# Twenty feed-forward chunks on ScalarE and GpSimd instead of nine, and one written order for the whole loop

## The chip, the cores and the metric

The kernel runs on one core of one Trainium2 chip. Its time is that of one execution on the device, in microseconds (us). The engines are named as in the profile: PE is TensorE with PEld its weight loads, DVE is VectorE, ACT is ScalarE, POOL is GpSimd, and SP is SyncE, which here only issues DMAs.

## The reference

```python
# x: 4 x 12416 x 128, inducing: 32 x 128, d_ff = 1536
def mab(q, kv):                       # softmax attention, scale 1/sqrt(128)
    s = scale * (q @ kv.transpose(0, 2, 1))
    s = s - s.max(-1, keepdims=True)
    a = np.exp(s)
    a /= a.sum(-1, keepdims=True) + 1e-09
    return a @ kv
h = mab(I, x)                         # stage 1: 32 inducing rows look at all 12416 rows
y = mab(x, h)                         # stage 2: every row looks at the 32 rows of h
gate = 1.0 / (1.0 + np.exp(-(y @ w_gate)))
out = (gate * (y @ w_val)) @ w_out    # feed-forward with a sigmoid gate
```

## The kernel before

Each of the four batches has 97 columns of 128 rows. They are cut into six groups of 16 columns and one spare column. Stage 2 is never multiplied out to 128 wide rows: h is folded into the two input weights (the tile `hw`), so the feed-forward part reads the attention weights themselves. A group's attention weights, normalised and copied four times along the partitions, are `a2n`; a transposing DMA issued on SP turns them into `a2r`, from which PE works.

The feed-forward work is cut into 97 blocks of 512 rows (24 to a batch, and one of the spare columns) and every block into 12 chunks of 128 hidden units. A chunk on its usual way needs: two matmuls with 32 rows of contraction, for the gate (`g_ps`) and for the value (`v_ps` or `vm_ps`); on ACT a tanh of the gate into a ring of 16 chunks (`issue_gate`, L1162; the sigmoid is half of one plus the tanh of half the input); on DVE one instruction that makes u = (tanh + 1) * value (`product`, L1350); and four matmuls of u with the output weights that add into `acc_ps` (`out_mm`, L1248). ACT scales each finished block into `o32` (L1273) and SP writes it out. PSUM has room for one gate tile of two chunks (tag g2), one of one chunk (g1), and for the values the tile v2 and the tile `vm` with two banks each, used in turn. The second bank of `vm` (tag m) is lent to everything else: scores, sums and folds of the stages for later groups and for the next batch.

A chunk that is set aside does not pass DVE: ACT takes the tanh (`gate_take`, L1211) and copies the value out of PSUM (`value_take`, L1216), and POOL adds one (L1213) and multiplies (L1218). The table `ASIDE` lists nine such chunks, all in the last batch. For a group of stage 2, ACT copies the scores (L688), POOL finds the maximum and subtracts it (`s2_lower_pool`), ACT takes the exponential `e` (L712), and POOL adds (L720), inverts (L744 and three more) and spreads (`a2n`, L766).

The order of the work comes from two places. The string `ORDER` is a list of words: g issues the gate of two chunks or of one, in strict turn; V or W the values; x a product; o a number of output matmuls; p, a and d run the oldest waiting side step on PE, ACT or DVE. Which side steps wait there, and when, is decided by the tables `TIMES` and by `turn_page`, which looks at due positions as the chunks advance; steps on POOL, loads and SP's DMAs are issued as soon as they are due. Each engine then runs its instructions in the order in which they were issued.

Of the kernel before, what the change touches and what calls it, by code (L numbers as in the profile page):

```python
# [53 lines left out]
WIDE, FULL, NARROW = "128x32", "128x128", "32x128"  # L54
NEXT = "the slot behind"
RING = 16
ORDER = """
ggVxgVxpgpVxgo4gVd0xo4Vxgo12Vxgo4ggVxo8a0gVxo4Vxgo12Wxa0ggVxo12gWxo4gVxo4go4Vxgo4gVxpVxgo8pa0gVx
gVxo12Vxa0gpVd0xgo16a0gVxo8gWxo4ggVxo4Wxgo8gVxo8Vxa0ggpo8Vd0xga0gVxo16gVxo4Wxgo8gVxo12a0gWxgo12g
Vxo4pa0gVxo4pa0gVxo8gWxo8Vxgo4gWxo8a0gVxgo12gWxo4go4gVxo4pgVxo4pVxa0go8gWxo12Vxa0gVxgpo4gVd0xo4V  # L60
xgo4go8Vxa0go8gWxo8gVxo4go4pgVxpVxo4a0a0ggWxo8gVxo8gVxpo4gVd0xo4Vxgo4go8Vxa0go12Wxa0gVxgo8pa0gVd
0xo12a0gVxo4gVxo12pVd0xgo8gWxo4a0ggVxo12pVxgpgVxo12a0gVxo4gVxo4pgVxo4pVxa0go12Wxa0gVxgo12VxgpgVd
0xo4Vxgo20Vxa0ggWxo12Vxa0ggo4pVxgo4pgVxo4Vxgo12Vxa0go8gWxo4go4gVxo8a0gVxpgVd0xo8a0gVxo12Vxa0go8p
Vxa0go4gVxo8pgVxpVxa0go8a0gWxVxgo12pgVxo4pgVxo4a0gVxo12gVd0xo4pVxa0go12Vxa0gWxgo12gVxo4go4pgVxpa
1gVxo8a0gWxo8Vxgo12a0gWxgo8Vxgo8gWxo8gVxo4go4Vxgo4gVxo12Vxa0ggVxo8gVxo8Vxa0ggVxo12Vxgo4gVxo4pgVd
0xo8Vd0xgo4a0ggVxpVxpo8a0gVxo8gWxo8gVxgo12gWxo12a0gVxgVxpo8a0gVxo4gVxo8gVxo4gWxo4go8gVxo4Wxgo8a0
ggVxo12gWxo4gVxo8gWxo8Vxa0ggo12pVxo4a0a0gVxgWxo8go4gVxo8gWxo4go4gVxo8gWxo12a0gVxgo8Wxgo8gVxo8gpg
VxpVxgo8a0gVxo4gVxo12Wxa0ggVxo16gWxo8Vxgo4ggWxo8gVxo12a0gVxgo4Vxgo8gWxo8gVxo8a0ggWxo16VxgWxo4a0g
gVxo12gWxo4go4Vxgo8gWxgo8gVxo4Vxgo8Vxa0gpVxgo8pa0gVxo12gWxo4gVxo8go4gWxo12a0gVxgpo8Vd0xgo8Vxa0go
4Wxgo4Vxgo8gWxo4go8gVxo4Vxa0gpgo12Vd0xga0gVxo8Vxgo4Wxgo8gVxo4gpVxpa0gVxgo12Wxa0gVxgo16pa0gVxo4gV  # L70
xpo8a0gVxgVxo8gWxo4Vxgo8a0ggWxo16gVxo4pgVxo4pVxa0go4Wxgo8gVxo12pa0gVd0xgo12a0gVxo12gWxgVxo8ggWxo
8gVxo8Vxa0gpgo8Vd0xVxgo4go8Vxa0go12WxggVxo16pVxa0gpVxa0go12gWxo12Vxa0gVxgo8pgVd0xo4a0gVxo8pgVd0x
o4a0ggWxo12gVxo4pgVxo4pVxa0go4Wxgo8ggVxo8pgVxo4pVxo4a0a0ggWxo8gVxo4gVxpo4gVd0xo4Vxgo20Vxa0ggWxo8
a0gVxgo8pVd0xgo8Vxa0go8Vxgo12gVxo8pVxgo4Vxa0a0gWxgo12gVxo12pa0gVxpgVxo12a0gVxo4gVxo8pa0gVxpgVxo8
a0gVxo8gVd0xo4po4a0gVxo4gVxo8Wxgo4gVxo8a1gWxgo12gVxo4gpVxpVxa1go4Wxgo4go8a0gVxo8gWxo8a0gVxgo12Vx
ggVxo12gWxo4Vxgo8gVxo12Vxa0ggVxo12Vxa0go4Vxgo8gVxo4VxgpgVd0xo4gVd0xo16Vxa0gpgVxo8pa0gVxo8Vxgo8Vx
go4Vxgo8gVxpVxa0go12Vxa0gWxgo12Vxgo4go4gWxo4Vxgo8go4gWxo4Vxgo8a0ggWxo12Vxgo4gWxo4gVxo12a0gWxgo16
# [12 lines left out]
Vxo8a0gWxgo4Vxa0go8Wxgo12gVxo4go4pa0gVxo4gVxo4Wxo8a0gVxgo12Wxgo4gVxgo8gWxgo8gVxo4Wxgo12Vxa0ggo4p  # L90
Vxpo4a0gVxo8Wxgo4go4gVxo4pVxa0go8gVxo12a0gWxgVxo12Wxgo8go4gVxo4pa0gVxo8Vxgo12Wxa0gVxgo20a0gWxgo8
Vxgo8Wxgo4gVxo8a0ggWxo12gVxo8pVxa0go4gVxo4Vxgo8gVxgVxo12a0gVxpVxgo8pa0gVxo12gVxo4gVxVxgo8pa0gVxo
4gVxo12Vxa0gVxgo12Vxgo4Vxgo8gVxpa0gVxo12gVxo12a0gWxVxgo20a0gVxgVxo4Vxgo4gVxgo8gWxo12Vxa0gWxgo8go
8gVxo4pVxgo4pVxa0go8gVxo4gVxo12Wxa0gVxgo12gWxo4go4gVxo8go4gWxo4Vxgo4gWxo8a0ggVxo12gWxo8gVxo8a0gW
xgo20Vxa0gpa0gVxo8Vxgo4gWxo8go4gVxo4Wxgo4Vxgo4ggVxo12Vxa0gpVxo4po4a0gVxgo8Wxgo8gVxo4pa0gVxo8Vxgo
12Wxa0gVxgo12pVxa0go4gVxo4gWxo4go4Vxgo8gWxo12a0gVxgo12a0gWxo8gVxo12pa0gVxo4gVxo8Vxgo4a0gVxgVxo12
gVxo4Vxgo4gVxpa0gVxo12gVxo4Vxgo12Vxa0ggVxo12gVxo8Vxgo4gVxpa0gVxo12gVxo8gVxo4a0gVxgVxo12gVxo4gVxp
o8a0gVxo4gVxo8gVxo4Vxgo8a0ggVxo12Wxgo8gVxo4Vxgo8pa0gVxo4Vxgo12a0gVxWxgo12Vxgo4go4pVxgo4a0gVxo4Vx
go8VxgVxgo12Vxa0gpa0gVxo20gVxVxpo12a0gVxgo12Vxgo4Vxa0ggVxo12VxgpVxgo8a0gVxo4gVxo12VxgVxgo12Vxa0g
Wxgo12Vxgo4go8gWxo8Vxgo4gVxgo12Vxa0ggVxo12VxgVxgo8gVxpa0gVxo12gVxo4Vxgo12Vxa0gVxgo16Vxo12Vxo4Vxo  # L100
16
# [4 lines left out]
def kernel(  # L106
# [49 lines left out]

    def x_load(b, s, first=()):
        c0, n = groups[s]
        if s == 0:
            c0, n = 0, n + NLO  # L160
        if b not in xn:
            xn[b] = xnp.tile([P, NCH, C], F16, tag="xn", name=f"xn_{b}")
        cuts = [c0, *(c0 + k for k in first), c0 + n]
        for c, e in zip(cuts, cuts[1:]):
            nc.gpsimd.dma_start(xn[b][:, c:e, :], xv[b, :, c:e, :])
# [125 lines left out]

    def on(what, i, besides=()):
        if vm:
# [10 lines left out]
    side = {"used": 0}  # L304
# [15 lines left out]
    def side_tile(shape, dtype, name):  # L320
        side["used"] += 1
        return bank("m", shape, dtype, name)

    def side_done():
        side["used"] -= 1

    summed = [0] * B
    sums, heads = {}, {}
# [10 lines left out]
    agenda, errands = [], []  # L339
# [5 lines left out]
    def errand(b, at, do):  # L345
        errands.append((b, at, do))
# [98 lines left out]
    def plan_stage1(b, s, score, *total):  # L445
        st = {}
        full = groups[s][1] == GC
        first, second, keep = total
# [29 lines left out]
        n = 512 if full else P  # L478
        if full:
            scores = chain(  # L480
                b - 1,
                (score, "take", fill, WIDE, n),
                (None, "dve", lambda: s1_max(b, s, st["s1"]), n),
# [959 lines left out]
```

## Time and profile before

| | |
|---|---|
| median of 3 runs | 716.03 us (715.92 to 716.07) |
| span of the profiled execution | 714.0 us |
| PE / PEld busy | 682.8 / 402.9 us |
| DVE busy | 698.2 us, 773 instructions |
| ACT busy | 678.0 us, 1019 instructions |
| POOL busy | 444.9 us, 718 instructions |
| granted TensorE clock, mean | 0.998 |

The span runs from the first to the last instruction of the program. The profile gives no other time of that execution; the median of the runs is 2.0 us above its span. A busy time is the union of the instructions' own durations, and consecutive instructions on one engine overlap in the records, so that the distance from one start to the next is often shorter than a duration.

### The profile page before, as it was taken

Reading aid. Unit: us, or ns where it says so; the run is one execution under the profiler, and the core shown is the slowest. Engines: PE = TensorE matmul, PEld = TensorE weight load, DVE = VectorE, ACT = ScalarE, POOL = GpSimd, SP = SyncE. Lnnn points to the kernel's source line nnn. Section 1 sums busy time; section 2 is a strip of 40 time slices with the busy share of each in tenths; the row PEclk is TensorE's granted clock in tenths of the full one; section 3 lists DMA queues with packets and bytes.
Section 4 is the critical chain, followed back from the end, with each engine's and each line's share of the span. In section 5 each row is a group of like instructions: output and inputs, shape, how many; then the busy total and the mean of one; then the engine's idle time right before and its main releaser. Section 6 shows DMA issues by size and latency. Waiting matters only on the chain. (4 is left out here: it accounts for less than half of the span.)

```text
span 714.0 us, 21196 instructions
## 1 busy us (share of the span) xinstructions
PE 682.8 (96%) x8446; PEld 402.9 (56%) x8446; DVE 698.2 (98%) x773; ACT 678.0 (95%) x1019; POOL 444.9 (62%) x718
## 2 busy tenths in 40 slices
PE   7899999999999999999999999999999999999997
PEld 4455565555555655555555555555555555555555
DVE  6899999999999999999999999999999999999997
ACT  4699999999999999999999999999999999999996
POOL 4574663788763747578766366378767787676220
PEclk9999999999999999999999999999999999999999
DMA  9797776244468353225258532220222222023011
GB/s 209 117 173 138 145 142 112 75 91 107 89 125 172 65 119 84 68 75 122 50 130 156 113 76 55 66 75 32 77 61 43 77 62 76 30 76 77 31 45 46
DMA packets 118179, 65.74 MB, mean 92 GB/s; under 512 B 101408, under 2 KB 102208, under 8 KB 118080
## 3 DMA queue, kind: packets, MB, share of 16 engines
q1 hardware_dynamic: 112176, 50.90, 29.9%
q0 software_dynamic: 5584, 13.34, 11.3%
q8 instruction: 66, 1.08, 0.7%
q14 instruction: 33, 0.27, 0.1%
q10 hardware_dynamic: 320, 0.15, 0.1%
HBM read 27.80 MB, written 25.43 MB: 75 GB/s over the span
## 5 line engine op out<-in xcount | busy, mean ns | idle before, releaser
L1162 ACT ACTIVATE t<-g_ps 128x1024 f16<-128x1024 f32 (+1 forms) x770 | 588.6, 821 | 14.5 <-ACT t L1162 2.8
L1350 DVE SCALAR_TENSOR_TENSOR u<-t,v_ps 128x1024 f16<-128x1024 f16 (+1 forms) x337 | 407.6, 1210 | 1.5 <-PE v_ps L1121 0.3
L1248 PE MATMUL acc_ps<-wo,u 128*128 128x128 f16 x4596 | 363.8, 220 | 4.7 <-DVE u L1350 0.7
L1248 PEld LDWEIGHTS <-u 128*128 128x128 f16 x4620 | 263.2, 98 | 153.2 <-issue 146.0
L1350 DVE SCALAR_TENSOR_TENSOR u<-t,vm_ps 128x1024 f16<-128x1024 f16 (+1 forms) x335 | 307.7, 919 | 0.8 <-issue 0.2
L1121 PE MATMUL g_ps<-a2r,hwt 32*128 32x512 f16 (+1 forms) x1179 | 287.8, 375 | 6.9 <-ACT t L1162 0.8
L1121 PEld LDWEIGHTS <-hwt 32*128 32x128 f16 x2382 | 99.3, 91 | 118.1 <-issue 48.4
L1121 PE MATMUL v_ps<-a2r,hwt 32*128 32x512 f16 (+1 forms) x687 | 129.3, 373 | 4.6 <-DVE u L1350 2.9
L1121 PE MATMUL vm_ps<-a2r,hwt 32*128 32x512 f16 (+1 forms) x492 | 129.6, 376 | 4.1 <-DVE u L1350 2.8
L720 POOL TENSOR_TENSOR sum<-e 128x256 f32<-128x256 f16 (+1 forms) x23 | 15.5, 672 | 122.9 <-ACT e L712 119.5
L766 POOL TENSOR_TENSOR a2n<-e,rs 128x2048 f16<-128x2048 f16 (+3 forms) x25 | 86.8, 3473 | 5.1 <-DVE rs L738 3.4
L744 POOL TENSOR_TENSOR near<-sme,minus 128x16 f32<-128x16 f32 (+1 forms) x22 | 65.2, 2964 | 1.7
L1273 ACT ACTIVATE o<-acc_ps 128x512 f32<-128x512 f32 x96 | 57.9, 604 | 0.1
L699 POOL TENSOR_SCALAR rise<-rise 128x256 f32<-128x256 f32 (+6 forms) x110 | 51.0, 464 | 9.7
L698 POOL TENSOR_TENSOR rise<-sc 128x256 f32<-128x256 f32 (+1 forms) x22 | 16.3, 739 | 27.5 <-ACT sc L688 27.5
L700 POOL TENSOR_TENSOR top<-top,rise 128x128 f32<-128x128 f32 (+3 forms) x88 | 28.3, 322 | 7.3
L720 POOL TENSOR_TENSOR sum<-sum 128x128 f32<-128x128 f32 (+3 forms) x92 | 28.3, 307 | 7.2
L698 POOL TENSOR_TENSOR rise<-top 128x128 f32<-128x128 f32 (+3 forms) x88 | 27.2, 309 | 6.9
L1218 POOL TENSOR_TENSOR xn_spare<-xn_spare 128x512 f16<-128x512 f32 x9 | 11.4, 1269 | 22.9 <-ACT xn_spare L1216 22.7
L1213 POOL TENSOR_SCALAR xn_spare<-xn_spare 128x512 f32<-128x512 f16 x9 | 13.4, 1490 | 18.8 <-ACT xn_spare L1211 18.7
L703 POOL TENSOR_TENSOR sc<-sc,top 128x512 f32<-128x512 f32 (+1 forms) x22 | 23.9, 1084 | 1.7
L651 PE MATMUL vm_ps<-hT,xT 128*128 128x32 f16 x376 | 17.5, 177 | 0.5 <-DVE u L1350 0.3
(165 smaller groups left out, 327.3 us busy)
## 6 DMA issues: line engine op xcount, KB each, us to landing
out_dram<-o SPq DMA_DIRECT2D x96, 256.0 KB, 2.3
xn<-in_x_dram POOLq DMA_DIRECT2D x18, 512.0 KB, 6.1
xn<-in_x_dram POOLq DMA_DIRECT2D x3, 544.0 KB, 6.4
xn<-in_x_dram POOLq DMA_DIRECT2D x3, 256.0 KB, 12.3
xn<-in_x_dram SPq DMA_DIRECT2D x1, 576.0 KB, 4.8
xn<-in_x_dram SPq DMA_DIRECT2D x1, 512.0 KB, 3.8
a2r<-a2n SPq DMA_TRANSPOSE x29, 4.8
wg<-in_moe_w_gate_dram POOLq DMA_DIRECT2D x1, 384.0 KB, 12.0
```

The costliest lines, as they stand in the source:

```text
L698: nc.gpsimd.tensor_tensor(out=r, in0=far, in1=near, op=ALU.subtract)
L699: nc.gpsimd.tensor_scalar_max(out=r, in0=r, scalar1=0.0)
L700: nc.gpsimd.tensor_tensor(out=top[:, 0:n, 0:w], in0=near, in1=r, op=ALU.add)
L703: nc.gpsimd.tensor_tensor(out=sc[:, 0:n, :], in0=sc[:, 0:n, :], in1=top[:, 0:n, 0:1].to_broadcast((P, n, m)), op=ALU.subtract,)
L720: nc.gpsimd.tensor_tensor(out=d[:, 0:n, :], in0=src[:, :, 0:w], in1=src[:, :, w : 2 * w], op=ALU.add)
L744: nc.gpsimd.tensor_tensor(out=near[:, 0:n], in0=sme[:, 0:n], in1=minus1[:, 0:n], op=ALU.pow)
L766: eng.tensor_tensor(out=a2n[:, 0:n, :, :], in0=e.unsqueeze(2).to_broadcast((P, n, 4, m)), in1=rs.unsqueeze(2).unsqueeze(3).to_broadcast((P ...
L1121: made_mm.append(nc.tensor.matmul(out[:, col : col + nb * P], hw[b][r : r + 32, j // 2, :], a2r[r : r + 32, o : o + nb, :].rearrange("p j ...
L1162: i = nc.scalar.activation(out=ring[:, p : p + n, :], in_=g[:, 0:n, :], func=AF.Tanh, scale=0.5)
L1248: mm = nc.tensor.matmul(acc[0][half][:, i, :], u[:, ts(i, P)], wo16[:, j, :], start=(i in fresh), stop=not left[ib] and not any(e[1] == ib ...
L1273: nc.scalar.mul(out=o32[:], in_=bank_[:], mul=0.5)
L1350: x = nc.vector.scalar_tensor_tensor(out=u[:, 0:n, a:e], in0=ring[:, p : p + n, a:e], scalar=1.0, in1=v[:, 0:n, a:e], op0=ALU.add, op1=ALU ...
```

## The change

Twenty chunks are set aside instead of nine: two in the first batch (blocks 2 and 10), three in the second (24, 31, 35), four in the third (50, 58, 59, 71), eleven in the fourth (75, 79 twice, 84, 86, 90, 91 three times, 95 twice). Before, the nine were in blocks 75, 79 twice, 86, 91 three times and 95 twice. The room that ACT and POOL need for them is taken from the tile of x that is loaded two batches later (`x_room`), and in the last two batches from a spare tile of that size.

`TIMES`, the agenda and `turn_page` are gone. Every side step, DMA and load belongs to a numbered chain, and the word k with its number runs the next step of that chain at that place. The word b does the same in the one-chunk gate bank g1 instead of bank m; twelve steps do so. The gate words are g for two chunks and h for one, in any turn. The word e scales a finished block on ACT, and f on DVE; there are 95 e and one f.

```diff
-ASIDE = {3: ((-1, 'm', 7, 'm', 3), (11, 'm', 17, 'm', 7), ...
-TIMES = (
...
+ASIDE = (
+    2, 10, 24, 31, 35, 50, 58, 59, 71, 75, 79, 79, 84, 86, 90, 91, 91, 91, 95, 95,
 )
...
-ggVxgVxpgpVxgo4gVd0xo4Vxgo12Vxgo4ggVxo8a0gVxo4Vxgo12Wxa0ggVxo12gWxo4gVxo4go4Vxgo4gVxpVxgo8pa0gVx
...
+gk0k0k0hVxVghxVxgo8Vho4xVgxVhk0o4xVgxo4Vhk72xo8gk74k0Vxo8hWo4xgVo8xehVk110gxo4Vk110k76ho8xVgo8xV
...
     def bank(tag, shape, dtype, name):
+        if tag == "m":
+            tag = here["bank"]
...
-    def chain(b, *steps, needs=()):
-        agenda.append(dict(b=b, steps=list(steps), at=0, name=len(agenda), needs=needs))
-        return agenda[-1]
+    def chain(*steps):
+        chains.append(dict(steps=list(steps), at=0, bank="m"))
+
+    def take_step(k, where):
+        w = chains[k]
+        step = w["steps"][w["at"]]
+        w["at"] += 1
...
     def issue_gate():
-        n, c, thin = units[gate["unit"]], gate["chunk"], gate["unit"] % 2
+        n, c = units[gate["unit"]], gate["chunk"]
+        assert n == 2 or not side["g1"]
...
     def side_room(b):
-        if b == B - 1:
+        if b >= B - 2:
             return spare_room()
-        t = sp.tile([P, 512], F16, tag="side_t", name="side_t", bufs=4)
...
+        if b not in rooms:
+            flat = x_room(b + 2)[:, NCH - 2 * GC :, :].rearrange("p j c -> p (j c)")
...
-        def evacuate():
-            nc.scalar.mul(out=o32[:], in_=bank_[:], mul=0.5)
+        def evacuate(mul):
+            mul(o32[:], bank_[:], 0.5)
             nc.sync.dma_start(ov[b, :, c : c + nb, :], o32[:])
...
-    def turn_page(c):
...
-        elif word == "g":
+        elif word in "gh":
             issue_gate()
...
+        elif word == "e":
+            evac.pop()(lambda out, in_, by: nc.scalar.mul(out=out, in_=in_, mul=by))
+        elif word == "f":
+            evac.pop()(lambda out, in_, by: nc.vector.tensor_scalar_mul(out=out, in0=in_, scalar1=by))
         else:
-            run(later[{"p": "pe", "a": "act", "d": "dve"}[word]].pop(int(k or 0)))
+            take_step(int(k), "m" if word == "k" else "g1")
```

Three places show how the order moves. The first is POOL near the start of the loop, in the first batch, where the weights of the group that begins with block 4 are made. `e`, `sme`, `rs` and `a2n` are that group's tiles, `xn_91` is the x of the second batch that is being loaded. Before:

```order
L720 TENSOR_TENSOR sum_771<-sum_769 128x16
L726 TENSOR_SCALAR sme<-sum_771 128x16
L165 DMA xn_91<-in_x_dram 128x2048 x2
L766 TENSOR_TENSOR a2n<-e,rs 128x2048
L698 TENSOR_TENSOR rise<-sc 128x256
```

Now, with `xn_834` the room of the chunk that is set aside:

```order
L695 TENSOR_TENSOR sum_764<-sum_762 128x16
L701 TENSOR_SCALAR sme<-sum_764 128x16
L1182 TENSOR_SCALAR xn_834<-xn_834 128x512
L160 DMA xn_91<-in_x_dram 128x2048
L1187 TENSOR_TENSOR xn_834<-xn_834 128x512
L741 TENSOR_TENSOR a2n<-e,rs 128x2048
L160 DMA xn_91<-in_x_dram 128x2048
```

Two POOL steps of the set-aside chunk now stand ahead of `a2n`, and one of the two loads has moved from ahead of `a2n` to just behind it.

The second place is POOL in the first batch where the weights for block 12 are made; `xn_1805` and `xn_834` are the x of the third batch, under its number in each program. Before:

```order
L726 TENSOR_SCALAR sme<-sum_1899 128x16
L744 TENSOR_TENSOR near<-sme,minus_132 128x16
L748 TENSOR_TENSOR off<-sme,near 128x16
L751 TENSOR_SCALAR off<-off 128x16
L759 TENSOR_TENSOR rs<-near,off 128x16
L766 TENSOR_TENSOR a2n<-e,rs 128x2048
L165 DMA xn_1805<-in_x_dram 128x2048
```

Now:

```order
L701 TENSOR_SCALAR sme<-sum_2045 128x16
L160 DMA xn_834<-in_x_dram 128x2048
L719 TENSOR_TENSOR near<-sme,minus_132 128x16
L723 TENSOR_TENSOR off<-sme,near 128x16
L726 TENSOR_SCALAR off<-off 128x16
L734 TENSOR_TENSOR rs<-near,off 128x16
L741 TENSOR_TENSOR a2n<-e,rs 128x2048
L1182 TENSOR_SCALAR xn_834<-xn_834 128x512
L1187 TENSOR_TENSOR xn_834<-xn_834 128x512
```

The load that stood just behind `a2n` now stands ahead of the inversion, and the steps of the chunk set aside in block 10 follow `a2n`.

The third place is ACT in the second batch, from the exponential `e` of the group that begins with block 28; `xn_4075` is the room of the chunk set aside in block 24. Before:

```order
L712 ACTIVATE e<-sc 128x512
L1162 ACTIVATE t_621<-g_ps 128x1024
L1162 ACTIVATE t_621<-g_ps 128x512
L1162 ACTIVATE t_621<-g_ps 128x1024
L1273 ACTIVATE o_4126<-acc_ps 128x512
```

Now:

```order
L687 ACTIVATE e<-sc 128x512
L1125 ACTIVATE t_621<-g_ps 128x1024
L1125 ACTIVATE t_621<-g_ps 128x512
L1180 ACTIVATE xn_4075<-vm_ps 128x512
L1125 ACTIVATE t_621<-g_ps 128x1024
L1185 COPY xn_4075<-side_v_ps 128x512
L1326 ACTIVATE o_4118<-acc_ps 128x512
```

Between the same neighbours ACT now takes the tanh and the value of one chunk that DVE would have multiplied.

More of the change, by code (lines that the diff above doesn't have):

```diff
@@ L155, with x_room @@
     xn, xT = {}, {}
+    def x_room(b):
+        if b not in xn:
+            xn[b] = xnp.tile([P, NCH, C], F16, tag="xn", name=f"xn_{b}")
+        return xn[b]
     def x_load(b, s, first=()):
@@ L160, in x_load @@
             c0, n = 0, n + NLO
-        if b not in xn:
-            xn[b] = xnp.tile([P, NCH, C], F16, tag="xn", name=f"xn_{b}")
+        x_room(b)
         cuts = [c0, *(c0 + k for k in first), c0 + n]
@@ L290 @@
     OTHER = {"v1": "m", "m": "v1"}
+    here = {"bank": "m"}
     def on(what, i, besides=()):
-        if vm:
+        if vm and (what != "m" or here["bank"] == "m"):
             me = str(i.ins.engine)
@@ L443, in s1_sum_keep, with plan_stage1 @@
         on("m", nc.scalar.copy(out=hsts[b % 2][0:R, at_col[s], 0:width], in_=hp[0:R, 0:width]))
-    def plan_stage1(b, s, score, *total):
+    def plan_stage1(b, s):
         st = {}
         full = groups[s][1] == GC
-        first, second, keep = total
         def fill():
@@ L476, in put, with most @@
             side_done()
[L478 removed]
+        def most():
+            s1_max(b, s, st["s1"])
         if full:
[L480 to L483, printed above, removed]
[L484 to L502 removed]
+            chain((fill,), most, weigh, turn_dma)
+            chain((lambda: part(0, 2),), lambda: part(2, 4), put)
+        else:
+            chain((fill,), most, weigh, turn_pe, turn_copy)
+            chain((lambda: part(0, 2),), put)
     hT16 = {}
@@ L558, in join_min, with plan_combine @@
         return top
[L560 removed]
+    def plan_combine(b):
         q = b % 2
@@ L624, in take @@
             side_done()
-        heads[b] = chain(
-            b - 1,
-            (lead, "dve", least, 60),
-            (None, "do", meet, 3000),
-            (weights, "act", weigh, 60),
-            (weights + 1, "do", join, 4600),
-            (weights + 8, "take", total, FULL, 640),
-            (None, "dve", invert, 60),
-            (None, "dve give", take, 60),
-            *(
-                step
-                for hf, (first, second) in enumerate(fill)
-                for step in (
-                    (first, "take", lambda hf=hf: part(hf), WIDE, 384),
-                    (None, "act give", lambda hf=hf: keep(hf), 384),
-                )
-            ),
-            needs=[(w, len(w["steps"])) for w in sums[b]],
+        chain(
+            least, meet, weigh, join, (total,), invert, take,
+            *(f for hf in range(2) for f in ((lambda hf=hf: part(hf),), lambda hf=hf: keep(hf))),
         )
@@ L783, in s2_turn_dma, with plan_stage2 @@
             a2[(b, c + j)] = (a2r, j)
-    def plan_stage2(at, b, c, score, take, weigh, far=None, soon=False):
+    def plan_stage2(b, c, far=False, soon=False):
         st = {}
-        n = GC + (NLO if far is not None else 0)
+        n = GC + (NLO if far else 0)
         def room():
@@ L806, in lower @@
         def lower():
-            if far is None:
+            if not far:
                 room()
@@ L1109 @@
     total_chunks = len(chunks)
-    units = []
-    while sum(units) < total_chunks:
-        units.append(min(1 + (len(units) + 1) % 2, total_chunks - sum(units)))
-    base = [b * NG * GC // BC * NJ for b in range(B)]
     def hidden_mm(what, c, out):
@@ L1373 @@
     for b in range(B):
-        more = b + 1 < B
-        times = TIMES[min(b, 1) if more else 2]
         if b == 0:
-            plan_stage2(0, 0, groups[1][0], 0, None, 3, soon=True)
-        for s, (*slots, far) in times["late"].items():
-            plan_stage2(b, b, groups[s][0], *slots, far=far)
-        for n, (g, gb, v, vb, i) in enumerate(ASIDE.get(b, ())):
-            k = sum(e[-1] == i for e in ASIDE[b][:n])
-            i += b * NG * GC // BC
-            plan_aside(b, g, v, i, beyond[i][k])
-        if not more:
+            plan_stage2(0, groups[1][0], soon=True)
+        for s in range(2, NG):
+            plan_stage2(b, groups[s][0], far=s == NG - 1)
+        if b + 1 == B:
             continue
-        for s, slots in enumerate(times["sum"]):
-            plan_stage1(b + 1, s, *slots)
-        plan_combine(b + 1, *times["join"][:2], times["join"][2:])
+        for s in range(NS):
+            plan_stage1(b + 1, s)
+        plan_combine(b + 1)
         for s in range(2):
-            plan_stage2(b, b + 1, groups[s][0], *times["next"][s])
+            plan_stage2(b + 1, groups[s][0])
+    for b in range(B - 1):
         for g in range(NS):
-            errand(b, times["turn"][g], lambda b=b, g=g: x_transpose_dma(b + 1, g))
+            chain(lambda b=b, g=g: x_transpose_dma(b + 1, g))
             if b == 0 and 0 < g < NG:
-                errand(b, (None, 4, 5, 17, 24, 31)[g], lambda g=g: x_load(1, g))
+                chain(lambda g=g: x_load(1, g))
         if b + 2 < B:
             for g in range(NG):
-                when = ((24, 33, 42, 60, 60, 82) if b else (33, 37, 60, 60, 78, 82))[g]
-                errand(b, when, lambda b=b, g=g: x_load(b + 2, g))
+                chain(lambda b=b, g=g: x_load(b + 2, g))
+    for n, i in enumerate(ASIDE):
+        plan_aside(i, beyond[i][ASIDE[:n].count(i)])
     for word, k in words:
@@ L1409 @@
                 out_mm()
-        else:
-            run(later[{"p": "pe", "a": "act", "d": "dve"}[word]].pop(int(k or 0)))
-    assert not queue and not agenda and not errands and not any(later.values())
+        elif word == "e":
+            evac.pop()(lambda out, in_, by: nc.scalar.mul(out=out, in_=in_, mul=by))
+        elif word == "f":
+            evac.pop()(lambda out, in_, by: nc.vector.tensor_scalar_mul(out=out, in0=in_, scalar1=by))
+        else:
+            take_step(int(k), "m" if word == "k" else "g1")
+    assert not queue and not evac and all(w["at"] == len(w["steps"]) for w in chains)
 _INS = ['x', 'inducing', 'moe_w_gate', 'moe_w_val', 'moe_w_out']
```

261 lines of the change are left out of this document (95 added, 166 removed).

## The prediction

> **What bounds the kernel now.** I read the page's busy times first, then the busy time by stretches, then the rows of the engine that is full, and last what it waits for.
>
> ```profile
> span 714.0 us, 21196 instructions
> ...
> PE 682.8 (96%) x8446; PEld 402.9 (56%) x8446; DVE 698.2 (98%) x773; ACT 678.0 (95%) x1019; POOL 444.9 (62%) x718
> ```
>
> Three engines are above 94%, so the mean does not decide. The stretches do (start and end in us, length, then the busy time of each engine):
>
> ```profile
> 30.00:42.00 12.00, 11.41 (x125) 6.20 (x123) 11.56 (x14) 11.46 (x17) 6.61 (x12) 1.00 0.73 142
> 42.00:651.00 609.00, 589.49 (x7298) 348.28 (x7298) 608.20 (x631) 595.87 (x888) 411.52 (x664) 1.00 0.42 91
> 651.00:693.00 42.00, 40.73 (x453) 23.26 (x449) 41.25 (x46) 41.25 (x62) 12.04 (x9) 1.00 0.22 53
> 693.00:714.00 21.00, 16.71 (x255) 11.49 (x255) 16.89 (x20) 14.27 (x22) 1.27 (x1) 0.93 0.14 51
> ```
>
> From 42 to 651 us DVE is idle for 0.8 us in all, PE for 19.5 and ACT for 13.1. So DVE sets the pace there. From 651 to 693 DVE and ACT are equally full. Nearly all of DVE's time is the product, in three shapes; and from start to start a product of two chunks takes 1.13 us (110.40 to 111.53) and one of one chunk 0.60 us (109.80 to 110.40), less than the durations, since records overlap:
>
> ```profile
> L1350 DVE SCALAR_TENSOR_TENSOR u<-t,v_ps 128x1024 f16<-128x1024 f16 x335 | 406.8, 1214 | 1.5 <-PE v_ps L1121 0.3 <-ACT t L1162 0.3 <-PE g_ps L1121 0.2
> L1350 DVE SCALAR_TENSOR_TENSOR u<-t,vm_ps 128x1024 f16<-128x1024 f16 x149 | 181.1, 1215 | 0.3 <-issue 0.2
> L1350 DVE SCALAR_TENSOR_TENSOR u<-t,vm_ps 128x512 f16<-128x512 f16 x186 | 126.7, 681 | 0.4 <-PE vm_ps L1121 0.2
> ...
> 109.80 0.68 DVE L1350 SCALAR_TENSOR_TENSOR u<-t,vm_ps 128x512 f16<-128x512 f16 x1
> 110.40 1.21 DVE L1350 SCALAR_TENSOR_TENSOR u<-t,v_ps 128x1024 f16<-128x1024 f16 x1
> 111.53 1.22 DVE L1350 SCALAR_TENSOR_TENSOR u<-t,vm_ps 128x1024 f16<-128x1024 f16 x1
> ```
>
> The idle columns add up to 2.2 us for 670 products. There is next to nothing to win from waits on DVE; only less work on it helps.
>
> **DVE's work.** Eleven more chunks leave the products: 1155 chunks become 1144. Counted in the two written orders, products of two chunks go from 484 to 479 and those of one chunk from 187 to 186. That is 5 x 1.13 + 0.60 = 6.25 us less. One finished block is scaled on DVE instead of ACT. The nearest row has half its width, and the 512-wide product has its width:
>
> ```profile
> L1265 DVE TENSOR_SCALAR o<-vm_ps 128x256 f32<-128x256 f32 x1 | 0.4, 425 | 0.3 <-PE vm_ps L1248 0.3
> ```
>
> Between 0.4 and 0.7 us; I take the 0.60 of the one-chunk product, from start to start. It is on the path, since DVE is full, and the products behind it on DVE stand while it waits for the block's last output matmul; that matmul stands just ahead of it in the written order, so a wait of up to one product (1.1 us) is possible, and I put none. DVE's net is 6.25 - 0.60 = 5.65 us. What hides everything else is that DVE stays the fullest engine, and this has to be checked for ACT, POOL and PE.
>
> **ACT's work.**
>
> ```profile
> L1162 ACT ACTIVATE t<-g_ps 128x1024 f16<-128x1024 f32 x385 | 397.5, 1032 | 14.0 <-ACT t L1162 2.8 <-PE v_ps L1121 1.2 <-PE vm_ps L1121 0.7
> L1162 ACT ACTIVATE t<-g_ps 128x512 f16<-128x512 f32 x385 | 234.4, 609 | 0.5 <-PE g_ps L1121 0.2
> L1273 ACT ACTIVATE o<-acc_ps 128x512 f32<-128x512 f32 x96 | 57.9, 604 | 0.1
> L1211 ACT ACTIVATE xn_spare<-vm_ps 128x512 f16<-128x512 f32 x9 | 5.4, 602 | 0.0
> L1216 ACT COPY xn_spare<-vm_ps 128x512 f32<-128x512 f32 x9 | 5.3, 593 | 0.0
> ```
>
> Eleven more chunks cost a tanh and a copy each, 11 x (602 + 593) ns = 13.1 us. The usual tanhs become 386 of two chunks and 372 of one: 1.03 us more and 13 x 609 ns = 7.9 us less. One scaling goes, 0.6 us. The net is 5.6 us by durations. ACT is busy for 662.9 us of the 684 between 30 and 714 us (the four stretches above added); with 5.6 us more in 5.65 us less it would be at 98.5%, below DVE's. By starts it is further from full: of the rows
>
> ```profile
> 698.06 0.60 ACT L1273 ACTIVATE o<-acc_ps 128x512 f32<-128x512 f32 x1
> 698.54 4.19 ACT L1162 ACTIVATE t<-g_ps 128x1024 f16<-128x1024 f32 x5
> ```
>
> the first has a duration of 0.60 us and its successor starts after 0.48. So I take ACT's work as hidden, and price its failure as a rival. In the last batch, where ACT and DVE are equal, only two of the eleven new chunks lie.
>
> **PE and SP.** PE has the same matmuls in both programs, and switches between matmuls of 32 and of 128 rows less often (1344 runs of one shape before, 1274 now). Its cost is nil if DVE paces; if PE paces, nothing is won, a rival below.
>
> [...]
>
> ```profile
> L1213 POOL TENSOR_SCALAR xn_spare<-xn_spare 128x512 f32<-128x512 f16 x9 | 13.4, 1490 | 18.8 <-ACT xn_spare L1211 18.7
> L1218 POOL TENSOR_TENSOR xn_spare<-xn_spare 128x512 f16<-128x512 f32 x9 | 11.4, 1269 | 22.9 <-ACT xn_spare L1216 22.7
> ...
> 315.00:336.00 21.00, 20.59 (x241) 12.25 (x239) 21.00 (x26) 20.54 (x31) 19.35 (x25) 1.00 0.50 103
> 378.00:399.00 21.00, 20.32 (x265) 12.13 (x261) 21.00 (x24) 20.52 (x32) 7.58 (x17) 1.00 1.03 184
> ...
> L1350 DVE SCALAR_TENSOR_TENSOR u<-t,v_ps 128x1024 f16<-128x1024 f16 x12 | 14.5, 1210 | 0.0
> L1350 DVE SCALAR_TENSOR_TENSOR u<-t,v_ps 128x1024 f16<-128x1024 f16 x11 | 13.4, 1214 | 0.0
> ```
>
> POOL gets 11 x (1490 + 1269) ns = 30.4 us more and goes from 445 to 475 us, two thirds of the span. As an engine it has room. It could slow DVE beside it: but with POOL busy for 19.35 of 21 us the two-chunk product took 1210 ns (first of the last two rows), and with POOL busy for 7.58 of 21 us it took 1214 ns (second). So the added POOL work costs the products nothing. [...]
>
> **Order on POOL and the weights of the next group.** Here the change can add a wait. PE's first gate of a group needs `a2r`, which lands after e on ACT, 10 us on POOL and a transposing DMA on SP. PE runs in order, so a late `a2r` holds the values behind it too, and DVE then has at most the product whose values stand in the other PSUM tile, 1.13 us, before it stands. Three places in the first half are tight:
>
> ```profile
> 84.27 0.71 PE L1121 MATMUL g_ps<-a2r,hwt 32*128 32x512 f16 x3
> 74.78 5.19 SPq L777 DMA_TRANSPOSE a2r<-a2n  x1
> a2r<-a2n SPq DMA_TRANSPOSE x1, 7.6
> ...
> 113.95 0.39 PE L1121 MATMUL g_ps<-a2r,hwt 32*128 32x512 f16 x2
> 104.40 0.64 POOL L165 DMA_DIRECT2D xn<-in_x_dram  x1
> 104.49 6.01 SPq L777 DMA_TRANSPOSE a2r<-a2n  x1
> a2r<-a2n SPq DMA_TRANSPOSE x1, 9.3
> ...
> a2r<-a2n SPq DMA_TRANSPOSE x29, 4.8
> ...
> 30.36 1.22 DVE L1350 SCALAR_TENSOR_TENSOR u<-t,v_ps 128x1024 f16<-128x1024 f16 x1 [0.27 <-ACT t L1162]
> 709.01 0.75 DVE L1350 SCALAR_TENSOR_TENSOR u<-t,v_ps 128x384 f16<-128x384 f16 x2
> ```
>
> For block 8 the DMA was issued at 74.78 and landed 7.6 us later, at 82.4; the first gate ran at 84.3. For block 12 it landed at 104.49 + 9.3 = 113.8 us, 0.15 us ahead of the gate. Both were slower than the median of 4.8 us; for block 12 the row of POOL shows a load of x issued just ahead. DVE needs 0.59 us for a chunk (679 us from its first product at 30.4 to its last at 709.8, over 1155 chunks). Now, counted in ACT's written order:
>
> - Block 8: between its e and its first gate stand 31 chunks, not 36. That is 2.9 us less time, with a load behind `a2n` as before: 1.9 - 2.9 = -1.0 us.
> - Block 12: 29 chunks, not 34, so 2.9 us less, and 0.64 us for the load that now stands ahead of the inversion. But that load is then out of the way: at 4.8 us instead of 9.3 us the result is 0.15 - 3.5 + 4.5 = +1.1 us; if the DMA is slow all the same, -3.4 us.
> - Block 4: POOL now does the chunk's two steps first. The value is copied 20 chunks (11.8 us) ahead of the first gate; the copy, the multiplication and `a2n` (0.59 + 1.27 + 3.61 us, the last from the row below) leave 6.3 us for the DMA, +1.5 us at 4.8 us and -3.0 us at 9.3 us, since a load now follows `a2n` directly.
> - Block 44: 34 chunks, not 37, and a load directly behind `a2n`; the DMA was issued at 331.97, took 5.1 us to land and the gate ran at 339.42. So 2.3 - 1.8 = +0.5 us, or -3.7 us at 9.3 us.
>
> ```profile
> 331.97 3.62 SPq L777 DMA_TRANSPOSE a2r<-a2n  x2
> a2r<-a2n SPq DMA_TRANSPOSE x2, 5.1
> 339.42 0.39 PE L1121 MATMUL g_ps<-a2r,hwt 32*128 32x512 f16 x2
> 43.04 3.61 POOL L766 TENSOR_TENSOR a2n<-e,rs 128x2048 f16<-128x2048 f16 x1 [1.43 <-DVE rs L738]
> ```
>
> The ends are 0 (all in time, or covered by the 1.13 us) and 1.0 + 3.4 + 3.0 + 3.7 = 11.1 us. Most terms lie near the good end, so I take 1.0 us.
>
> **The sum.** Against the profiled execution: 714.0 - 6.25 + 0.60 + 1.0 = 709.35 us of span. The median of the runs, 716.03, lies 2.0 us above that span, and I keep the 2.0: 711.4 us, 4.65 us or 0.65% less. The difference that a measurement of this kernel can tell from none is about 0.2%, 1.4 us: faster means below 714.6, slower above 717.5.
>
> **Rivals.**
>
> 1. *Late weights (slower).* The mechanism is the one above: with POOL's steps and loads moved, the first gates of blocks 4, 8, 12 and 44 find no `a2r`, PE stands, and DVE with it. At the full price it is 716.03 - 5.65 + 11.1 = 721.5; with half of it covered, 716. It decides from 7.1 us on (5.65 + 1.4). For it: 0.15 us of room at block 12 before. Against it: other groups gain room in the same count (block 32: 45 chunks, not 33).
> 2. *ACT becomes the bound in the last batch.* There ACT had no less to do than DVE (41.25 us each of 42). Its two new chunks save DVE 2 x 0.57 us to no use and cost ACT 2 x 1.195 less two halves of 1.03, 1.4 us; with as much again for the crowded stretch ahead: 716.03 - 5.65 + 1.1 + 2 x 1.4 = 714.3. For it: from 651 to 693 us ACT is idle for only 0.75 us. Against it: starts closer than durations, and gates that now run further ahead of the products (on average 2.7 to 3.5 chunks in the last 160 products, not 1.8 to 2).
> 3. *PE paces and DVE only looks full.* PE is at 589.49 of 609 us. Then the time stays at about 716. Against it: DVE's idle time, 0.8 us in 609.
> 4. *POOL holds up DVE.* If each added POOL instruction held DVE for half its length, 15.2 us: 716.03 - 5.65 + 15.2 = 725.6. The 1210 and 1214 ns speak against it. [...]
> 5. *More than forecast:* no late weights, and the 0.75 us of DVE's idle time from 651 to 693 goes too: 716.03 - 5.65 - 0.75 = 709.6, with a cheaper scaling 709.
>
> **How the numbers follow.** Forecast 0.60 (709.5 to 713.5); late weights 0.16, half of it within 0.2% and half slower; ACT 0.12, mostly still faster (0.10 and 0.02); PE 0.05 (0.04 same, 0.01 slower); POOL 0.03 (0.02 slower, 0.01 same); more than forecast 0.04. That makes 0.74 faster, 0.15 same, 0.11 slower. The likeliest case gives 711.4. The range runs from 708.8, below rival 5, to 716.6, where some 0.12 lies above and little below.
>
> **What the changed profile would show.** DVE's products: 479 and 186, some 6.8 us less busy, with idle time between 42 and 690 us still below 2 us; that is the forecast. PE waiting on the DMA of `a2r`, with idle DVE beside it near 57, 83, 112 or 335 us, is rival 1. ACT without gaps while DVE waits for its tanh in the last 100 us is rival 2. DVE idle throughout, with PE full, is rival 3; a two-chunk product of clearly more than 1215 ns is rival 4. A time above 714.6 would make the prediction wrong.

## The result, and the profile after

The kernel after takes 744.7 us in the median, where 711.4 was forecast; against the kernel before it is 1.041 times as long (95% interval 1.039 to 1.044). Two of its six runs, 755.2 and 759.0 us, are slow ones at a mean granted clock of 0.950 and 0.941, and the median, the ratio and all differences below go by the other four (742.2 to 750.3 us; the median of all six is 748.0). The granted clock is the share of TensorE's full speed that the profile records as granted. The profiled execution is the 743.7 us one, with a span of 741.8 us. The top of its page:

```profile
span 741.8 us, 21216 instructions
...
PE 688.7 (93%) x8446; PEld 403.2 (54%) x8446; DVE 697.3 (94%) x768; ACT 681.8 (92%) x1028; POOL 475.8 (64%) x740
```

The span grew by 27.8 us. None of the three full engines got that much work (POOL did, 30.9 us, but it is busy for 64% only); all three have idle time. Where it lies is seen in the stretches of the kernel after (start and end in us, length, busy time of each engine, granted clock, DMA share, GB/s):

```profile
42.00:63.00 21.00, 15.68 (x181) 8.66 (x179) 16.31 (x19) 15.52 (x24) 15.35 (x22) 0.94 0.78 132
63.00:84.00 21.00, 20.46 (x250) 11.97 (x247) 18.82 (x19) 19.22 (x29) 8.73 (x11) 0.90 0.62 118
84.00:105.00 21.00, 16.88 (x179) 9.05 (x176) 14.66 (x16) 14.32 (x22) 9.13 (x19) 0.76 0.79 138
105.00:126.00 21.00, 19.89 (x278) 12.31 (x278) 20.91 (x26) 20.83 (x34) 14.93 (x17) 1.00 0.86 78
126.00:147.00 21.00, 16.46 (x152) 8.68 (x150) 11.89 (x13) 11.89 (x18) 6.18 (x16) 0.59 0.48 78
147.00:168.00 21.00, 18.49 (x273) 11.00 (x270) 18.98 (x22) 18.64 (x31) 16.97 (x34) 1.00 0.53 114
357.00:378.00 21.00, 18.64 (x193) 10.63 (x189) 17.97 (x18) 17.94 (x27) 14.60 (x28) 0.84 0.50 96
...
42.00:651.00 609.00, 568.70 (x6988) 332.90 (x6986) 579.07 (x595) 571.33 (x854) 415.50 (x653) 0.97 0.43 88
651.00:693.00 42.00, 40.43 (x465) 23.41 (x466) 41.82 (x45) 41.63 (x63) 31.22 (x37) 1.00 0.29 65
```

The third busy time is DVE's. From 42 to 651 us it is idle for 29.9 us, where it was 0.8 before; 27.5 of these lie in the seven short stretches shown, six of which lie ahead of 168 us. In five of them the granted clock is below 1.0, down to 0.59; before it was 1.00. From 651 to 693 us DVE is as full as it was.

What PE waited for in it (total in us, times, longest):

```profile
PE g_ps L1082 <- DMA a2r<-a2n: 12.0, 5, 4.5
...
PE vm_ps L376 <- DMA xT<-xn: 4.9, 1, 4.9
```

And from its timeline four of these waits (in brackets), with issues of DMAs ahead of them:

```profile
50.13 0.59 POOL L160 DMA_DIRECT2D xn<-in_x_dram  x1
50.21 5.48 SPq L752 DMA_TRANSPOSE a2r<-a2n  x1
55.79 3.24 SPq L169 DMA_TRANSPOSE xT<-xn  x1
61.16 0.62 PE L376 MATMUL vm_ps<-xT,indT 128*32 128x512 f16 x4 [4.86 <-DMA xT<-xn]
61.84 0.69 DVE L388 TENSOR_REDUCE nm<-vm_ps 128x1 f32<-128x512 f32 x1 [4.69 <-PE vm_ps L376]
...
84.56 0.64 POOL L160 DMA_DIRECT2D xn<-in_x_dram  x1
85.11 7.23 SPq L752 DMA_TRANSPOSE a2r<-a2n  x1
95.27 0.61 PE L1082 MATMUL g_ps<-a2r,hwt 32*128 32x512 f16 x2 [3.95 <-DMA a2r<-a2n]
...
120.81 9.20 SPq L752 DMA_TRANSPOSE a2r<-a2n  x1
132.09 0.61 PE L1082 MATMUL g_ps<-a2r,hwt 32*128 32x512 f16 x2 [4.54 <-DMA a2r<-a2n]
...
366.69 0.39 PE L1082 MATMUL g_ps<-a2r,hwt 32*128 32x512 f16 x2 [1.16 <-DMA a2r<-a2n]
```

At 61 us PE waits for `xT`, whose transposition stood in SP's queue behind a turn of weights that took 5.48 us to issue. At 95, 132, 167 (1.93 us) and 367 us it waits for the turned weights of blocks 8, 12, 16 and 44. These five stands (idle time of PE ahead of something late) add up to 16.4 us. With four of them the clock is halved: in the trace's record of it, it is 0.5 for 6.83 us from 60.40, for 10.24 us from 94.53, for 17.07 us from 128.67 and for 6.83 us from 367.60, 41.0 us in all. (The last microseconds of each execution, where the clock falls as well, to 0.5 from 711.2 us on before and from 739.7 us on in the kernel after, are left out in this and in all that follows.) In the row at 95.27 a gate matmul takes 0.61 us, where the same at full clock takes 0.39 (the last row).

How long the turns (the transposing DMAs from `a2n` to `a2r`) that are issued from 45 to 200 us take to land, in the median:

```profile
a2r<-a2n SPq DMA_TRANSPOSE x6, 8.9
```

And the same stretch of the kernel before:

```profile
a2r<-a2n SPq DMA_TRANSPOSE x7, 5.8
```

DVE's products, by shape:

```profile
L1269 DVE SCALAR_TENSOR_TENSOR u<-t,v_ps 128x1024 f16<-128x1024 f16 x332 | 402.9, 1214 | 6.3 <-PE v_ps L1082 3.2 <-PE g_ps L1082 2.1
L1269 DVE SCALAR_TENSOR_TENSOR u<-t,vm_ps 128x1024 f16<-128x1024 f16 x147 | 178.3, 1213 | 9.8 <-PE vm_ps L1082 7.0 <-PE g_ps L1082 2.1 <-ACT t L1125 0.2
L1269 DVE SCALAR_TENSOR_TENSOR u<-t,vm_ps 128x512 f16<-128x512 f16 x185 | 125.8, 680 | 9.4 <-PE vm_ps L1082 7.1 <-PE g_ps L1082 0.8 <-ACT o L1326 0.7
```

The work did go down as counted: 479 products of two chunks, 7.6 us less busy, each as long as before. From the start of the first product to the end of the last DVE takes 707.1 us instead of 679.4. If each of its instructions is counted at its usual (median) time from start to start, the work in this is 6.2 us less and the waiting 33.9 us more (40.2 instead of 6.3). That is the whole change: 33.9 - 6.2 = 27.7 us.

### The profile page after: what moved, and what is told of

Read it like the earlier page. It is cut to its first block, busy times and chain, and to the rows that moved or that the text cites. A ratio compares the mean times of both kernels' runs of the same rounds, so it can differ in the third digit from the quotient of the medians.

```text
span 741.8 us, 21216 instructions
## 1 busy us (share of the span) xinstructions
PE 688.7 (93%) x8446; PEld 403.2 (54%) x8446; DVE 697.3 (94%) x768; ACT 681.8 (92%) x1028; POOL 475.8 (64%) x740
## 4 chain that ended last, share of the span: by engine, by line
PE 44%; ACT 23%; DVE 10%; DMA 10%; issue 7%; POOL 5%; DVEq 0%; ACTq 0%; SPq 0%; POOLq 0%
PE acc_ps L1211 21%; ACT t L1125 18%; PE g_ps L1082 11%; DVE u L1269 9%; DMA a2r<-a2n 7%; PE v_ps L1082 5%; PE vm_ps L1082 4%; ACT o L1326 2%; DMA xn<-in_x_dram 2%; POOL a2n L741 2%; POOL near L719 1%; DMA xT<-xn 1%; POOL xn L160 1%; PE vm_ps L376 1%; ACT e L687 1%
## 5 line engine op out<-in xcount | busy, mean ns | idle before, releaser
L1269 DVE SCALAR_TENSOR_TENSOR u<-t,v_ps 128x1024 f16<-128x1024 f16 x334 | 403.7, 1209 | 6.3 <-PE v_ps L1082 3.2
L1211 PEld LDWEIGHTS <-u 128*128 128x128 f16 x4576 | 267.2, 99 | 152.2 <-issue 147.4
L1269 DVE SCALAR_TENSOR_TENSOR u<-t,vm_ps 128x512 f16<-128x512 f16 (+1 forms) x332 | 304.2, 916 | 19.2 <-PE vm_ps L1082 14.1
L1082 PEld LDWEIGHTS <-hwt 32*128 32x128 f16 x2360 | 94.7, 91 | 140.5 <-issue 64.0
L1182 POOL TENSOR_SCALAR xn_spare<-xn_spare 128x512 f32<-128x512 f16 x15 | 22.4, 1494 | 25.4 <-ACT xn_spare L1180 25.3
L1187 POOL TENSOR_TENSOR xn_spare<-xn_spare 128x512 f16<-128x512 f32 x15 | 19.0, 1269 | 27.1 <-ACT xn_spare L1185 26.6
L673 POOL TENSOR_TENSOR rise<-top 128x128 f32<-128x128 f32 (+3 forms) x88 | 27.3, 310 | 6.9
L388 DVE TENSOR_REDUCE nm<-vm_ps 128x1 f32<-128x512 f32 (+1 forms) x21 | 13.1, 626 | 5.2 <-PE vm_ps L376 5.1
```

The lines of the kernel that those rows point to most:

```text
L673: nc.gpsimd.tensor_tensor(out=r, in0=far, in1=near, op=ALU.subtract)
L1082: made_mm.append(nc.tensor.matmul(out[:, col : col + nb * P], hw[b][r : r + 32, j // 2, :], a2r[r : r + 32, o : o + nb, :].rearrange("p j ...
L1211: mm = nc.tensor.matmul(acc[0][half][:, i, :], u[:, ts(i, P)], wo16[:, j, :], start=(i in fresh), stop=not left[ib] and not any(e[1] == ib ...
L1269: x = nc.vector.scalar_tensor_tensor(out=u[:, 0:n, a:e], in0=ring[:, p : p + n, a:e], scalar=1.0, in1=v[:, 0:n, a:e], op0=ALU.add, op1=ALU ...
```

## The experiments

Theory A: the turns of weights and the transposition behind one of them are late because loads of x are in flight beside them, and PE's stands cost their own length and a halved clock besides. Rival B: with twenty chunks set aside, POOL and ACT are too slow, and the loads are only seen beside it. Rival C: the halved clock costs nothing, since DVE is the bound.

**Seven loads moved.** Only words of the written order change place (k78, k84, k85, k86, k87, k88, k101 are loads of x; each now stands behind a tree of maxima on POOL):

```
- o8 k78 k1      + o8 k1 k78        - V k84 k2 k82 g   + V k2 k82 k84 g
- o4 k2 k85 x    + o4 k2 x ... k3 k85 h
- x k87 k86 k20  + x k20 ... k5 k87 k86 x
- o4 h k88 o8    + o4 h o8 ... k21 k88 o8
- x k101 k43 g   + x k43 k101 g
```

> Only the written order is changed: seven loads of x on POOL's queue, each of which stands right behind a spreading of weights (`a2n`) or a sum ahead of one, go behind the tree of maxima that follows, so that none is in flight while the weights of blocks 4, 8, 12, 16, 20 and 44 are turned by DMA. Theory A (the turns are late because a load of x is in flight beside them): the turns of `a2r` fall from 7.2-11.2 us between issue and landing to some 4.4 us, the waits of PE for `a2r` and `xT` (16.4 us in five stands) nearly vanish, the granted clock stays at 1.0 from 10 us to the end, and the time is 709 to 716 us. Rival B (POOL and ACT with twenty chunks set aside are themselves too slow, the loads are only seen beside it): the turns are issued as late as now and the time stays at 735 to 745 us.

Measured: 715.4 us, 0.999 of before (0.998 to 1.001), in the medians 29.4 us less than the kernel after. The turns issued from 45 to 200 us:

```profile
a2r<-a2n SPq DMA_TRANSPOSE x7, 4.4
```

The turn of block 8 in the timeline, with the loads that now follow it:

```profile
78.70 2.10 SPq L751 DMA_TRANSPOSE a2r<-a2n  x1
86.73 1.18 POOL L159 DMA_DIRECT2D xn<-in_x_dram  x2
```

And the stretch around that block's first gate:

```profile
84.00:105.00 21.00, 20.21 (x280) 12.35 (x278) 21.00 (x25) 20.79 (x33) 11.09 (x19) 1.00 0.84 154
```

The turns take 4.4 us and not 8.9, none is waited for, and DVE is full for all 21 us around block 8, which had 6.3 us of idle time. All twenty chunks are still set aside and POOL runs the same instructions. So the first half of A holds, the loads and the late turns, and B falls. The seven were moved together; the next two runs try one each. The clock is still halved once, for 6.83 us from 270.34, where no stand is longer than 0.41 us. Of ten runs the five with a mean clock of 1.0 took 713.8 to 714.7 us, the five at 0.993 to 0.996 took 716.0 to 718.2.

**One load moved.** Of the above only `o8 k78 k1` to `o8 k1 k78`, ahead of block 4.

> Only the first of those loads moves: the fourth group of batch 1, 0.08 us ahead of the turn for block 4, goes behind the tree. Theory A: the turn issued at 50.2 us lands in some 4.4 us and not 9.2, the transposition of `xT` queued behind it on SP lands 4 to 5 us earlier, PE's stand of 4.86 us ahead of 61.2 us and the 6.8 us of halved clock behind it go, and the others stay: 742 - (4.7 + 1.8 us of idle time of DVE) = about 735 us. Rival B: no change, 740 to 745 us.

Measured: 738.7 us, 1.031 of before (1.029 to 1.034). In its trace the turn at 49.57 us lands after 4.4 us, the stand for `xT` falls from 4.86 to 0.76 us and the clock holds up to 86 us; from 42 to 63 us DVE is busy for 20.30 us and not 16.31. The gain is 6.0 us in the medians, where 6.5 was expected. But the stands at blocks 8 and 12 grew to 4.66 and 4.82 us and the slow stretch behind the second from 17.1 to 27.3 us, so the stretches were not as independent as I had them.

**One load put back.** The order with the loads moved, but `V k84 k2 k82 g` as in the kernel after.

> The order with the seven loads behind the trees, and one of them put back: the first load of batch 2 stands again right behind the spreading of block 8's weights. Theory A: the turn of block 8 alone takes some 10 us again, PE stands about 4.5 us at its gate near 85 us, the clock is halved for 7 to 10 us there, and nothing else changes, since blocks 12 and 16 had 2.8 and 2.1 us of room: 714.4 to 715.4 + 5 to 7 = 719 to 722 us. Rival D (the lateness adds up over several loads and stands, one alone is covered): 714 to 717 us.

Measured: 721.7 us, 1.009 of before (1.007 to 1.011), 6.3 us more than with it moved. From its timeline:

```profile
77.72 0.64 POOL L159 DMA_DIRECT2D xn<-in_x_dram  x1
78.28 7.60 SPq L751 DMA_TRANSPOSE a2r<-a2n  x1
...
89.43 0.61 PE L1081 MATMUL g_ps<-a2r,hwt 32*128 32x512 f16 x2 [4.95 <-DMA a2r<-a2n]
```

How long that turn took to land, and then, as another view, the stretch:

```profile
a2r<-a2n SPq DMA_TRANSPOSE x1, 11.1
```

```profile
84.00:105.00 21.00, 15.86 (x152) 8.64 (x149) 13.69 (x17) 13.31 (x21) 3.91 (x10) 0.76 1.09 115
```

One load, issued 0.56 us ahead of one turn, makes it 11.1 us long instead of 4.4, PE stands for 4.95 us, the clock is halved for 10.24 us from 87.71, and DVE loses 7.3 us of the 21. Rival D falls: one alone is not covered.

**Idle matmuls in place of the waits.** In the kernel after:

```
+ for _ in range(FILL.get(c, 0)):
+     nc.tensor.matmul(g[:, 0, :], ident[:], wo16[:, 0:4, :], start=True, stop=True)
  for k in range(n):
      hidden_mm("g", c + k, g[:, k, :])
```

> The order of the kernel after, with idle matmuls for PE in place of the five waits: 22 matmuls of 512 columns ahead of the scores that wait for `xT` at 61 us, and 18, 20, 8 and 5 ahead of the first gates of blocks 8, 12, 16 and 44; each writes a bank that the real matmul behind it overwrites. The DMAs stay as late as they are. Theory A with the clock (a stand of PE of some microseconds halves the granted clock for 7 to 17 us and that costs as well as the wait): the clock stays at 1.0, DVE's idle time behind the waits (1.8, 1.2, about 4.5, 1.2 us) goes and only the waits stay: about 731 to 735 us. Rival C (the clock follows but costs nothing, since DVE is the bound and PE has room): 740 to 745 us, as the kernel after.

Measured: 746.7 us, 1.043 of before (1.041 to 1.045). This is a miss, and it decides nothing between A and C. With the first wait filled the clock held until 96.75 us, but block 8's weights landed at 95.20 us, as they had at 95.22 without, so PE still stood 2.16 us behind its 18 idle matmuls. A new stand of 3.23 us ended at 129.20 us, with the clock halved from 127.47; block 12's 20 idle matmuls, partly at the halved clock, ran until 136.7 us, 5.6 us past the landing of the weights at 131.1. Those for block 16 never ran, because no pair of gates starts at that chunk, and PE stood 4.07 us there. What it does show is that block 8's weights came no sooner although their turn was issued 2.2 us earlier (at 82.89 us, 85.11 without): the turn took 12.3 us instead of 10.1, and the time won ahead of it was waited away.

**Stands planted in the kernel before**, with everything else unchanged:

```
+ late = t_of[-2]
+ for k in range(STAND.pop(at)):          # 1, 2, 3 DMAs in a row
+     hop = xT[B - 2][:, 4 * k : 4 * k + 4, :].rearrange("p j t -> p (j t)")
+     nc.sync.dma_start(hop, late)
+     late = hop
+ nc.tensor.matmul(g[:, 0, :], ident[:], late, start=True, stop=True)
```

> The kernel before with three stands of PE planted in the last batch, where nothing else changes: ahead of the gates of chunk 880, 940 and 1010 a matmul reads a tile that comes by one, two and three DMAs in a row from the tanh that frees the gate's bank, so that PE waits some 2, 4 and 6 us. Theory A with the clock: the stand of 2 us costs 0 to 1 us and leaves the clock at 1.0, those of 4 and 6 us halve it for 7 us or more; in all 716 + 1 + (4 - 1) + (6 - 1) + 2 x 2 for the slow stretches = about 728 us. Rival C (no price of the clock): 716 + 0 + 3 + 5 = 724 us or less.

**PE held as long, but busy.** The same three gates, with 10, 17 and 24 idle matmuls and no DMA.

> The counterpart of the planted stands: at the same three gates of the kernel before, PE does not wait for DMAs but runs 10, 17 and 24 idle matmuls of 512 columns, 2.2, 3.7 and 5.2 us at 216 ns each, about as long as the stands were (2.1, 3.6, 5.3 us). PE is held as long, but it is busy. Theory A with the clock (a large part of the 20.7 us of the planted stands was the halved clock behind them): the clock stays at 1.0 and the time is 716 + 11.1 less some cover of 0 to 1 us at each = 724 to 727 us. Rival C (the clock behind a stand costs nothing, the time held is all): as the planted stands, 735 to 739 us.

Measured: with stands 736.7 us, 1.029 of before (1.027 to 1.032); busy 726.6 us, 1.015 (1.013 to 1.017). The stretches around the three stands in the first:

```profile
546.00:566.00 20.00, 17.88 (x145) 9.43 (x141) 12.35 (x12) 12.82 (x18) 11.87 (x19) 0.57 0.19 47
591.00:600.00 9.00, 6.26 (x47) 3.40 (x48) 3.39 (x5) 3.47 (x6) 5.05 (x11) 0.62 0.15 54
639.00:651.00 12.00, 9.66 (x79) 4.97 (x79) 4.23 (x5) 6.30 (x9) 2.52 (x4) 0.52 0.32 77
```

The first of these stretches in the second kernel:

```profile
546.00:566.00 20.00, 19.62 (x227) 11.43 (x225) 18.00 (x18) 17.87 (x27) 13.02 (x19) 1.00 0.23 60
```

PE stood 2.1, 3.6 and 5.3 us, 11.0 in all, and the median grew by 20.7 us; held for as long but busy it grew by 10.7 and the clock stayed at 1.0. The other 10 us go with the halved clock. How much that is for a microsecond has to be taken from the two profiled executions, since the halved stretches (17.07, 6.83 and 13.65 us, 37.55 in all) are those of the profiled one, which is the longest of the four with stands (739.6 us). Their spans, 737.8 and 724.9 us, differ by 12.9 us. Of these, 0.9 lie ahead of DVE's first product, where the first of them has another 3.41 us of halved clock. That leaves 12 us, 0.32 for each microsecond of halved clock; 10.2 us between the medians would give 0.27. Rival C falls. (The two kernels differ besides only in the six short DMAs that make the stands.) My expectation for the stands, 728 us, was too low too: I had the shortest of them leave the clock alone, and DVE lost 7.7 us of 20 behind it.

**Three more steps.** On top of the seven loads: `xT` of the second group ahead of the turn for block 4 (k73 behind k76), four output matmuls behind the next value and gate matmuls (`W g x o4 V h g` to `W g x V h o4 g`), and the one block back from DVE to ACT (`f` to `e`).

> The order with the seven loads behind the trees, and three steps more: `xT` of the second group of batch 1 is transposed some 9 us earlier, ahead of the turn for block 4 and not behind it (PE stood 0.7 us for it at 57 us); the one block that DVE scaled goes back to ACT (0.60 us); four output matmuls that waited 0.4 us for ACT at 267.7 us, where the granted clock was halved in some runs, go behind the next value and gate matmuls. If what is left of DVE's waits was these: 712.5 to 714 us, and no halved clock. If the small late arrivals of 0.1 us per 20 us are the rest, or ACT is full there: 714 to 715.5 us, as the runs with an even clock had before.

Measured: 714.7 us, 0.9995 (0.998 to 1.001), in the second of the two ranges expected; a span of 712.6 us and a clock of 1.0 in the profile. The stand at 57 us is gone, but DVE waits 1.45 us for gates near 620 us, where ACT took the block over. The same with that block on DVE:

> As the run before (seven loads behind the trees, `xT` ahead of the turn for block 4, four output matmuls later), but the one block stays scaled on DVE: with it on ACT, the gates near 620 us came late and DVE stood 1.45 us there, more than the 0.60 us it saved. If ACT is full there and that was the cause: DVE has 0.60 us more work and some 1.4 us less idle time, 0.8 us less in all, 713.5 to 714.2 us where the clock is even. If it was chance: 715 us, no better than with it on ACT.

Measured: 714.0 us, 0.998 (0.997 to 0.9998), 1.9 us under before in the medians. It is the one version whose interval lies below 1, and only just. It is as expected if ACT was full there, but the 0.7 us between this version and the last are no more than the spread of either's runs. From its page:

```profile
span 711.6 us, 21216 instructions
...
PE 673.4 (95%) x8446; PEld 397.3 (56%) x8446; DVE 695.4 (98%) x768; ACT 679.8 (96%) x1028; POOL 475.7 (67%) x740
```

And the long stretch:

```profile
42.00:651.00 609.00, 583.45 (x7323) 343.89 (x7321) 606.85 (x627) 599.17 (x900) 440.35 (x685) 1.00 0.42 91
```

## Why the prediction was wrong, point by point

**DVE's work: right.** 6.2 us less by starts, 5.65 forecast. It is there in the kernel after too, under 33.9 us of waiting.

**ACT, PE and POOL: right as far as the work goes.** ACT is busy for 3.8 us more, where I had worked out 5.6, and POOL for 30.9, where I had 30.4. DVE's waits for ACT in the kernel after come to 2.8 us by starts (1.2 before), and the two-chunk product takes 1214 and 1213 ns with 31 us more work on POOL (1214 and 1215 before). Half the length of POOL's added work as time lost on DVE, 15.2 us in rival 4, was my assumption; no run shows it, and the product did not get longer.

**The weights of the next group: this step failed.** I gave late weights two ends, 0 and 11.1 us, and took 1.0. Three things were wrong in it.

1. *The length of the turn.* I had the cause on the page: the two slow turns of before that I showed, 7.6 and 9.3 us, had a load of x issued 0.09 us ahead. For blocks 4 and 44 I even wrote that a load would now follow `a2n` directly. Still I let the median of all 29 turns, 4.8 us, most of which had no load in flight beside them, stand for most of them. They took 9.2 (block 4), 10.1 (8), 11.2 (12) and 9.1 us (44). At block 12 I had the load out of the way because it was issued earlier; it was issued at 112.61 us and took 16.0 us itself, so it was in flight all the same. Blocks 16 and 20 were not in my list; there loads stood ahead of the turns as well, and block 16 cost PE 1.93 us.
2. *What stands behind the turn on SP.* The transposition of `xT` for the scores at 61 us was queued behind block 4's turn. I listed the DMAs for the gates only; the longest stand, 4.86 us, was for this one. No gate waited for block 4's weights: they landed at 59.39 us, while PE stood for `xT`.
3. *The price of a stand.* I priced a stand of PE at its length less 1.13 us of cover. In this kernel four of the five also halved the clock. With 16.4 us of stands and 41.0 us of halved clock at the 0.27 to 0.32 us measured above, the estimate is 16.4 + 11 to 13, so 27 to 30 us, beside 28.6 us more idle time of DVE from 42 to 693 us. My full price for rival 1, 721.5 us, had neither the clock nor the stands for block 16 and for `xT`, and the range ended far below the result.

So the mechanism was in the main that of rival 1, which I had at 0.16: I had named waits near 57, 83, 112 and 335 us, and PE stood until 61 (for `xT`, not for block 4's weights), 95, 132 and 367. Each comes later for the most part by its own length and by what was lost ahead of it.

**The sum, with the weights in time.** The last version has the work I forecast, no late weights and, in the profiled execution, an even clock, and its span is 711.6 us, not the 708.35 that the sum gives without the 1.0 us for late weights. By starts, DVE's waiting in it is 9.9 us, 3.7 more than before, in many small waits for gates and values (110 longer than 15 ns in the version with that block on ACT, 64 before). I had taken ACT's work as hidden; ACT is at 599.2 of 609 us there, 595.9 before. That its fuller row makes these small waits is likely but was not tried by itself.

## What to carry to other kernels

Price a DMA by the rows that had the same company, not by the median of all: look at what else is in flight when it is issued and what is queued behind it on its engine. A stand of PE can cost more than its length (here 20.7 us for three of 11.0 us), so when a change moves loads in a written order, check for each transfer that something waits for how much room it has with the slow price. Where a change loses time in waits, its saving may still be there, and moving a few loads can bring it out.

## What the runs showed of the hardware

- The granted clock of TensorE fell to one half behind stands far shorter than I would have thought to matter: 2.1 us (the first planted stand) and 1.16 us (at 366.69 us in the kernel after), while 1.93 us at 167 us left it at 1.0. The halved stretches last 3.41, 6.83, 10.24, 13.65, 17.07 or 27.31 us, multiples of 3.41, and within one trace they begin a whole number of 3.41 us apart (94.53 - 60.40 is ten of them in the kernel after), so how a stand falls on that grid seems to matter; no run shifts a stand alone to show it. Of the 3.41 us ahead of a halving PE was idle, by the records, for only 0.7 us (ahead of 270.34 us with the seven loads moved) or 1.5 us (ahead of 367.60 us in the kernel after); of the 3.41 us ahead of 166.2 us in the kernel after, 31 such steps behind 60.40, it was idle for 1.25 us, and the clock stayed at 1.0. What decides between the two, no run here shows.
- A transposing DMA of 512 KB inside SBUF (`a2r` from `a2n`) took 4.4 us in the median of the turns with the loads moved, and 7.2 to 11.2 us in the kernel after, from block 4 on, where a load of x from DRAM (512 or 544 KB) was in flight beside it. A transposition of `xT` and a load issued 0.4 us apart took 18.2 and 16.0 us (at 112 us in the kernel after). Why one DMA slows the other so much, no run here shows.
